# Attention before a mixture of experts: values held stationary in 64-column tiles, softmax weights streamed, sums added up on VectorE

## The chip, the cores and the metric

The kernel runs on one core of one Trainium2 chip. The metric is the device time in microseconds of one execution; the time before is the median of three runs. Times inside the kernel come from one profiled execution.

## What is computed

Eight batches of 448 tokens, twelve heads of 64, then a layer of eight experts that gives each token to one of them; all in float32.

```python
# attention: q, k, v are (8, 12, 448, 64)
scores = scale * np.matmul(q, k.transpose(0, 1, 3, 2))
scores = cap * np.tanh(scores / cap)
scores = scores - np.max(scores, axis=-1, keepdims=True)
attn = np.exp(scores)
attn = attn / (np.sum(attn, axis=-1, keepdims=True) + 1e-09)
x = np.matmul(attn, v)                     # then laid out as (3584, 768)
# experts: w_gate (768, 8), w1 (8, 768, 1024), w2 (8, 1024, 768)
logits = x @ w_gate + modality_bias[modality_id]
e_idx = np.argmax(logits, axis=1)          # one expert a token
gate_w = softmax(logits)[token, e_idx]
out[e_idx == e] = gate_w * (np.maximum(x @ w1[e], 0) @ w2[e])
```

## The kernel before

**The work in stages.** The 96 heads are taken as 48 pairs (two heads of a batch; `NP` = 6 pairs a batch). `attention` (L420) runs over the pairs `g` in four steps each, then the experts follow. TensorE holds one operand of a product stationary (`LDWEIGHTS`, in the profile PEld) and streams the columns of the other. A plain float32 product is two records in the profile. A float32r product has one record; so that no precision is lost, an operand is split into a rounded high half (`kh`, `qs`, `qd`) and the rest (`kl`, `kd`, and the lower rows of `qs`), and their products are summed.

**Scores** (`scores`, L532, products at L547). The keys of a head are cut into three blocks of 128 and a last one of 64, and the two last blocks of a pair make a shared one, so a pair has seven units of 128 keys by 448 queries. Keys are stationary. `kr` and `qr` hold q and k twice, in rows 0 to 63 and 64 to 127, so that one product of 128 rows sums two of the terms (high times high, and high times the rest) and a second one adds the third. Three steps make two units each, the fourth step the shared one with three products: 15 products a pair. ScalarE applies tanh (L552) and exp (L553) to 896 columns, or 448 in the last step, into `pt`: 128 keys by 448 queries a unit.

**Values** (`weigh`, L555). One pair later, for each of four chunks of 112 queries: the chunk of `pt` is stationary and the values `va` are streamed, seven float32 products a step, 28 a pair. A row of `va` holds 64 values, 8 columns of gating values and a one, 73 columns in all (the shared unit, L558, streams both heads' 146). So the product gives the output rows, the head's part of the gating logits, and the softmax denominator beside each other. `normalize` (L575) takes four reciprocals of 112 rows (L579), multiplies the outputs into `xs` (L581) and the logits into `lg` (L587), twice a pair.

**Gating values.** For the values of later pairs `later_gate` (L461) multiplies each pair's transposed values `vt` with the gating weights, three pairs ahead; `put_gate_values` (L410) copies the result into `va`.

**The split of q and k** (`prep`, L491, for the next pair, in step 1): VectorE casts and subtracts (L507 to L517).

**Routing** (`route`, L187, at the end of each batch). VectorE adds up the logits of the 12 heads (L191), finds the largest, and counts: the rank of a token within its expert comes from two small products (`rank`, L218 and L219, the second with the sums `before` that the chain makes up to L215). From it come the positions `pos` (L229). GpSimd writes token number and weight `pay` (iota at L233) with four index DMAs a batch into the map `mapd` (L242). `pay` has two buffers (pool `rp`). GpSimd also stores every half batch of `xs` to `xd` (L658). The seventh routing also chooses the first expert (`early_slot`); at pair 44 its rows are fetched through the map (`mt`, L709; `xg`, L716). The first expert's weights are loaded and split between the last pairs' steps (`split_w`, L730: cast on ScalarE at L732, subtraction on VectorE at L733).

**What sets the order.** A planner orders each engine's instructions, except those that `self.pin` keeps where the code puts them. Before, the products of most pairs are free to move. All DMAs of GpSimd stand in one queue and are issued in order.

Of the kernel before, what the change touches and what calls it, by code (L numbers as in the profile page):

```python
# [42 lines left out]
VA = D + E + 1  # L44
KU, KR = 3, 64
NU = 2 * KU + 2
KW = 2 * S + KR
OWN = KU * 128
GE = 2 * E
# [11 lines left out]
HB = 3  # L61
GH = 2 * HB * GE


class Program:
    def __init__(self, tc, qT, kT, v, vT, cap, mod, wgb, mb, w1, w2, out):
        self.tc, self.nc = tc, tc.nc
        self.qT, self.kT, self.v, self.vT = qT, kT, v, vT
        self.cap, self.mod, self.wgb, self.mb = cap, mod, wgb, mb
        self.w1, self.w2, self.out = w1, w2, out  # L70
# [17 lines left out]
    def constants(self, cpool, dram):  # L88
# [6 lines left out]
        make_identity(nc, self.ident)  # L95
        self.capt = cpool.tile([128, 1], F32, name="capt")
# [12 lines left out]

        self.ones = cpool.tile([CP, 512], BF16, name="ones")  # L110
# [32 lines left out]
    def gate_weights(self):  # L143
        self.wgt = self.cpool.tile([128, NP, GE], F32, name="wgt")
        self.load(self.wgt.rearrange("p h e -> p (h e)"), self.wgb)
# [41 lines left out]
    def route(self, b, lg, pool, ps, tok=None):  # L187
# [3 lines left out]
        nc.vector.tensor_reduce(L, lg.rearrange("p c h e -> p c e h"), axis=AX.X, op=ALU.add)  # L191
# [191 lines left out]
    def load_qk(self, pool, g, parts=1):  # L383
        nc = self.nc
        b, hp = divmod(g, NP)
        kr = pool.tile([128, 2, S], F32, name="kr")
        qr = pool.tile([128, 2, S], F32, name="qr")
        step = 2 * S // parts
        for i in range(parts):
            cs = slice(i * step, (i + 1) * step)  # L390
            for t, src in ((kr, self.kT), (qr, self.qT)):
                self.load(t.rearrange("p j s -> p (j s)")[:, cs], src[b, hp][:, cs])
        return kr, qr

    def gate_values(self, vt, hp, ps, pin=False):

        vg = ps.tile([128, 512], F32, name="vg", tag="small")
        for c in range(KU + 1):
            n = slice(c * 2 * E, (c + 1) * 2 * E)
            for r in range(2 if c == KU else 1):  # L400
                m = slice(r * KR, (r + 1) * KR) if c == KU else slice(0, 128)
                keys = slice(c * 128, c * 128 + (KR if c == KU else 128))
                move = self.nc.tensor.matmul(
                    vg[m, n], vt[:, keys], self.wgt[:, hp], start=True, stop=True
                )
                if pin:
                    self.pin(move)
        return vg[:, : NU * E].rearrange("p (c e) -> p c e", c=KU + 1)

    def put_gate_values(self, va, vg):  # L410
        nc = self.nc
        nc.vector.tensor_copy(
            va[:, : 2 * KU, D : D + E].rearrange("p (c j) e -> p c j e", j=2),
            vg[:, :KU].rearrange("p c (j e) -> p c j e", j=2),
        )
        for j in range(2):
            rows = slice(j * KR, (j + 1) * KR)
            nc.vector.tensor_copy(va[rows, 2 * KU + j, D : D + E], vg[rows, KU, j * E : (j + 1) * E])

    def attention(self, qk, first):  # L420
        tc, nc = self.tc, self.nc
        with ExitStack() as st:
            kp = st.enter_context(tc.tile_pool(name="kp", bufs=1))
            ld = st.enter_context(tc.tile_pool(name="ld", bufs=2))
# [3 lines left out]
            rp = st.enter_context(tc.tile_pool(name="rp", bufs=2))  # L428
            ps_s = st.enter_context(tc.tile_pool(name="ps_s", bufs=2, space=PSUM))
            ps_o = st.enter_context(tc.tile_pool(name="ps_o", bufs=2, space=PSUM))  # L430
            ps_v = st.enter_context(tc.tile_pool(name="ps_v", bufs=1, space=PSUM))


            khs, kls, kds = [], [], []
            for i in range(2):
                kh = kp.tile([128, KW], F32R, name=f"kh{i}")
                kl = kp.tile([128, 2, OWN], F32R, name=f"kl{i}")
                kd = kp.tile([128, 2, KR], F32R, name=f"kd{i}")
                nc.gpsimd.memset(kh.bitcast(F32)[:, S : S + KR], 0.0)
                nc.gpsimd.memset(kd.bitcast(F32), 0.0)  # L440
                khs.append(kh)
                kls.append(kl)
                kds.append(kd)

            wg = kp.tile([128, NP, HB, 2, GE], F32R, name="wg")
            nc.gpsimd.memset(wg.bitcast(F32), 0.0)

            def split_gate():
                for i in range(HB):
                    hi, lo = wg[:, i::HB, i, 0], wg[:, i::HB, i, 1]  # L450
                    nc.vector.tensor_copy(hi, self.wgt[:, i::HB])
                    nc.vector.tensor_tensor(lo, self.wgt[:, i::HB], hi, op=ALU.subtract)

            vgts = [kp.tile([128, KU + 1, HB, GE], F32, name=f"vgt{i}") for i in range(NP // HB)]

            def load_vt(g):
                vt = ld.tile([128, S], F32, name="vt" if g >= HB else "vt0", bufs=2 if g >= HB else 1)
                self.load(vt, self.vT[g // NP, g % NP])
                return vt

            def later_gate(g, vt):  # L461

                hp = g % NP
                vh = sp.tile([128, S], F32R, name="vh", bufs=1)
                keep = self.pin if g < 6 else (lambda inst: inst)
                keep(nc.vector.tensor_copy(vh, vt))
                vl = sp.tile([128, S], F32R, name="vl", bufs=1)
                keep(nc.vector.tensor_tensor(vl, vt, vh, op=ALU.subtract))
                if hp % HB == 0:
                    self.vga = ps_v.tile([128, 512], F32, name="vga")  # L470
                last = hp % HB == HB - 1
                w = wg[:, hp].rearrange("p h t e -> p (h t e)")
                keep(nc.tensor.matmul(self.vga[:GH, :S], w, vh, start=hp % HB == 0, stop=False))
                keep(nc.tensor.matmul(self.vga[:GH, :S], w, vl, start=False, stop=last))
                if not last:
                    return

                vgs = sp.tile([GH, S + KR], F32, name="vgs", bufs=1)
                nc.vector.tensor_copy(vgs[:, :S], self.vga[:GH, :S])
                nc.vector.tensor_copy(vgs[:, S:], self.vga[:GH, OWN:S])  # L480
                tp = self.ps_r.tile([128, 512], F32, name="vgp", tag="small")
                for c in range(KU + 1):
                    nc.tensor.transpose(tp[:, c * GH : (c + 1) * GH], vgs[:, c * 128 : (c + 1) * 128], self.ident[:GH, :GH])
                nc.vector.tensor_reduce(
                    vgts[hp // HB].rearrange("p c h e -> p (c h) e"),
                    tp[:, : (KU + 1) * GH].rearrange("p (x t e) -> p x e t", t=2, e=GE),
                    axis=AX.X,
                    op=ALU.add,
                )

            def prep(g):  # L491
                b, hp = divmod(g, NP)
                kr, qr = first if g == 0 else self.load_qk(qk, g)
                va = ld.tile([128, NU, VA], F32, name="va", bufs=3)
                self.load(va.rearrange("p u d -> p (u d)"), self.v[b, hp])

                kh, kl, kd = khs[g % 2], kls[g % 2], kds[g % 2]
                qs = sp.tile([128, 2, S], F32R, name="qs")
                qd = sp.tile([128, S], F32R, name="qd")
                keep = self.pin if g < 2 else (lambda inst: inst)  # L500

                copy = (lambda out, in_: keep(nc.scalar.copy(out, in_) if g == 0 else nc.vector.tensor_copy(out, in_)))
                for jj in ((0, 1),) if g else ((0,), (1,)):
                    js = slice(jj[0], jj[-1] + 1)
                    for j in jj:
                        o = j * (S + KR)
                        keep(nc.vector.tensor_copy(kh[:, o : o + S], kr[:, j]))  # L507
                    copy(qs[:, js], qr[:, js])
                    keep(nc.vector.tensor_tensor(qs[D:, js], qr[D:, js], qs[D:, js], op=ALU.subtract))  # L509
                    for j in jj:  # L510
                        o, r = j * (S + KR + KR), j * KR
                        keep(nc.vector.tensor_tensor(kl[:, j], kr[:, j, r : r + OWN], kh[:, o : o + OWN], op=ALU.subtract))
                for j in range(2):
                    rows = slice(j * D, (j + 1) * D)
                    r, o = OWN * (1 - j), (OWN, S + KR)[j]
                    copy(qd[rows], qr[rows, j])
                    keep(nc.vector.tensor_tensor(  # L517
# [557 lines left out]
```

## Time and the profile before

| | |
|---|---|
| median of three runs | 1003.48 us (999.76 to 1004.63) |
| the profiled execution | 1003.47 us |
| its span | 1001.9 us, 17725 instructions |
| TensorE busy | 976.2 us (97%) |
| weight loads (PEld) | 941.6 us (94%) |
| VectorE busy | 628.6 us (63%) |
| ScalarE busy | 586.5 us (59%) |
| GpSimd busy | 132.9 us (13%) |
| value products L567, 2304 records | 254.6 us, 260 ns each |
| scores L547, keys high, 384 | 152.2 us, 416 ns each |
| attention's first score product | at 10.3 us |
| first score product of pair 47 | at 465.64 us |
| first transpose of the experts' rows | at 474.4 us |

How to read it: "us" beside an instruction is how long it lasted from start to end; successive products overlap, so the time that one costs is the distance to the next start. `[9.81 <-DMA ...]` after a row is the idle time of its engine before it, and what ended that. PE is TensorE's products, PEld its weight loads, DVE VectorE, ACT ScalarE, POOL GpSimd, SP the engine that issues the loads. An operand is written `out<-in`, in the program's names.

### The profile page before, as it was taken

Reading aid. Unit: us, or ns where it says so; the run is one execution under the profiler, and the core shown is the slowest. Engines: PE = TensorE matmul, PEld = TensorE weight load, DVE = VectorE, ACT = ScalarE, POOL = GpSimd, SP = SyncE. Lnnn points to the kernel's source line nnn. Section 1 sums busy time; section 2 is a strip of 40 time slices with the busy share of each in tenths; the row PEclk is TensorE's granted clock in tenths of the full one; section 3 lists DMA queues with packets and bytes.
Section 4 is the critical chain, followed back from the end, with each engine's and each line's share of the span. In section 5 each row is a group of like instructions: output and inputs, shape, how many; then the busy total and the mean of one; then the engine's idle time right before and its main releaser. Section 6 shows DMA issues by size and latency. Waiting matters only on the chain. (4 is left out here: it accounts for less than half of the span.)

```text
span 1001.9 us, 17725 instructions
## 1 busy us (share of the span) xinstructions
PE 976.2 (97%) x6628; PEld 941.6 (94%) x6628; DVE 628.6 (63%) x1632; ACT 586.5 (59%) x762; POOL 132.9 (13%) x150
## 2 busy tenths in 40 slices
PE   6999999999999999998999999999999999999996
PEld 4999999999999989997999999999999999998996
DVE  5788888878888688767854444343434344337763
ACT  4678778777778777787254434443434344335552
POOL 2001011020202002022242020202020202001100
PEclk8999999999999999998999999999999999999999
DMA  5555556566555647576386353635353545447750
GB/s 177 154 202 147 201 200 168 179 142 213 167 192 156 200 162 184 178 169 237 73 302 220 126 200 121 211 128 193 134 177 141 181 141 180 142 139 227 253 169 36
DMA packets 61160, 173.38 MB, mean 173 GB/s; under 512 B 10366, under 2 KB 17278, under 8 KB 61056
## 3 DMA queue, kind: packets, MB, share of 16 engines
q1 hardware_dynamic: 51968, 138.97, 44.2%
q0 software_dynamic: 8944, 33.10, 10.0%
q8 instruction: 56, 0.92, 0.4%
q14 instruction: 48, 0.39, 0.1%
q10 hardware_dynamic: 144, 0.00, 0.0%
HBM read 150.52 MB, written 22.69 MB: 173 GB/s over the span
## 5 line engine op out<-in xcount | busy, mean ns | idle before, releaser
L567 PE MATMUL po<-va,pt 128*112 128x73 f32 x2304 | 254.6, 260 | 0.0
L567 PEld LDWEIGHTS po<-va,pt 128*112 128x112 f32 x2304 | 249.9, 179 | 0.2
L552 ACT ACTIVATE th<-sc,isc 128x896 f32<-128x896 f32 x192 | 175.2, 913 | 100.3 <-PE sc L547 99.5
L553 ACT ACTIVATE pt<-th,cabs 128x896 f32<-128x896 f32 x192 | 181.7, 950 | 5.8
L780 PE MATMUL ph<-x,al 128*128 128x384 f32 (+2 forms) x528 | 166.3, 315 | 0.0
L802 PE MATMUL py<-bh,hh 128*128 128x384 f32 x464 | 159.3, 343 | 1.1 <-ACT hh L786 1.1
L547 PE MATMUL sc<-qs,kh 128*128 128x448 f32 x384 | 152.2, 416 | 7.6 <-DVE qs L509 7.6
L802 PE MATMUL py<-bh,hl 128*128 128x384 f32 x464 | 156.1, 336 | 0.0
L802 PE MATMUL py<-bl,hh 128*128 128x384 f32 x464 | 155.4, 335 | 0.0
L776 PE MATMUL ph<-x,ah 128*128 128x384 f32 x384 | 128.5, 335 | 0.7 <-DVE x L759 0.7
L777 PE MATMUL ph<-x,ah 128*128 128x384 f32 x384 | 128.6, 335 | 0.0
L733 DVE TENSOR_TENSOR bl<-raw,bh 128x768 fp32r<-128x768 f32 x88 | 81.2, 955 | 51.0 <-ACT bh L732 49.9
L547 PE MATMUL sc<-qs,kl 128*128 128x448 f32 x288 | 109.3, 380 | 0.1
L732 ACT CAST bh<-raw 128x768 fp32r<-128x768 f32 x88 | 70.4, 840 | 55.9 <-DMA raw<-in_w_dram 51.4
L780 PEld LDWEIGHTS ph<-x,al 128*128 128x128 f32 x528 | 99.5, 188 | 0.0
L807 ACT ACTIVATE ot<-py,mt 128x384 f32<-128x384 f32 x58 | 33.6, 580 | 103.2 <-PE py L802 55.2
L762 DVE TENSOR_TENSOR x<-ptr,x 128x384 fp32r<-128x384 f32 (+2 forms) x66 | 32.6, 518 | 96.8 <-ACT x L761 96.6
L733 DVE TENSOR_TENSOR al<-raw,ah 128x1024 fp32r<-128x1024 f32 x66 | 78.8, 1222 | 17.4 <-ACT ah L732 17.1
L802 PEld LDWEIGHTS py<-bh,hh 128*128 128x128 f32 x464 | 87.3, 188 | 1.5 <-ACT hh L786 1.4
L802 PEld LDWEIGHTS py<-bl,hh 128*128 128x128 f32 x464 | 87.3, 188 | 0.0
L802 PEld LDWEIGHTS py<-bh,hl 128*128 128x128 f32 x464 | 87.1, 188 | 0.1
L786 ACT ACTIVATE hh<-ph 128x384 fp32r<-128x384 f32 x64 | 30.6, 489 | 94.7 <-PE ph L780 94.7
(167 smaller groups left out, 1397.0 us busy)
## 6 DMA issues: line engine op xcount, KB each, us to landing
raw<-in_w_dram SPq DMA_DIRECT2D x66, 512.0 KB, 4.6
raw<-in_w_dram SPq DMA_DIRECT2D x88, 384.0 KB, 4.8
kr<-in_kT_dram SPq DMA_DIRECT2D x47, 448.0 KB, 3.4
qr<-in_qT_dram SPq DMA_DIRECT2D x47, 448.0 KB, 4.5
va<-in_v_dram SPq DMA_DIRECT2D x48, 292.0 KB, 3.7
vt<-in_vT_dram SPq DMA_DIRECT2D x48, 224.0 KB, 4.1
xd<-xs POOLq DMA_DIRECT2D x16, 672.0 KB, 5.4
mapd<-pay,pos POOLq DMA_INDIRECT x32, 5.3
```

The costliest lines, as they stand in the source:

```text
L547: move = nc.tensor.matmul(sc[:, i, :S], k, q, start=n == 0, stop=n == len(todo) - 1)
L552: nc.scalar.activation(th[:, :n], sc[:, :n, :S], AF.Tanh, scale=self.isc)
L553: nc.scalar.activation(pt[:, units[0] : units[0] + n], th[:, :n], AF.Exp, scale=self.cabs)
L567: nc.tensor.matmul(po[:CP, o0 + j * VA : o0 + (j + 1) * VA], pt[:, j * KU + i, qs_], va[:, 2 * i + j], start=False, stop=j == 1 and i == K ...
L732: a = self.nc.scalar.copy(hi, raw)
L733: b = self.nc.vector.tensor_tensor(lo, raw, hi, op=ALU.subtract)
L762: nc.vector.tensor_tensor(lo, pt[:, :w], hi, op=ALU.subtract)
L776: nc.tensor.matmul(ph[:, :w], hi[:, fs], self.x[:, k, 0, :w], start=first, stop=False)
L777: nc.tensor.matmul(ph[:, :w], hi[:, fs], self.x[:, k, 1, :w], start=False, stop=False)
L780: nc.tensor.matmul(ph[:, :w], lo[:, fs], self.x[:, k, 0, :w], start=False, stop=last)
L802: nc.tensor.matmul(py[:, :HALF], self.h[a][:, f, rows], self.w2s[f][c][:, cs], start=i == 0, stop=i == 3 * FC - 1,)
L807: nc.scalar.mul(ot[:, cs], py[:, :HALF], mt[:, t, 1:2])
```

## The change

The attention stage is rebuilt; the experts keep their code but for two details.

- **Load.** One packed tile a pair, `kq` (128 x 960): head 0 in rows 0 to 63, head 1 in rows 64 to 127; 3 x 128 own keys, 2 x 64 last keys (block-diagonal, the other half zero), 448 queries. The transposed values and the doubled copies of q and k are not loaded. `va` has 64 columns a unit (512 in all), without gating values and ones.
- **Split** (`prep`, L418 of the new kernel). From pair 2 on the high half `hi` is made by a DMA on GpSimd's queue that casts on the way (L428); VectorE makes `lo` by one subtraction of 960 columns (L432).
- **Scores** (L435). Three terms (high-high, low-high, high-low) in 64-row tiles, head 0 in the upper and head 1 in the lower half of the array, 448 columns each; the shared block takes full products. Two steps' products are issued together.
- **Values** (L468, L476). Values stationary: six products with 64 columns a head, in the two halves of the array's columns, and one of 128 columns for the shared unit; 448 columns of `pt` stream in float32. The result `xT` is transposed: features in rows, queries in columns.
- **Denominators.** VectorE adds up the units of `pt` (`add_up`, L448). One pair later `normalize` (L458) sums over the rows by two float32 products with ones, takes a reciprocal of 128 x 448 (L463) and multiplies (L465). `rows_out` (L479) turns the result back by four transposes and a copy into `xs` (L484).
- **Gating** (L486, L496). Every half batch three products of the normalized `xn` with the gating weights, in 32-column tiles; at the end of the batch a copy `gl`, four transposes `lt`, and `route` sums three values a logit instead of twelve.
- **Order and buffers.** All of attention's products are pinned. The loop is two pairs longer (weigh one pair later, normalize two). Pool `rp`, and `pay` with it, has one buffer instead of two. `den`, `tp`, `lt` and `rank` share one PSUM tile. The raw weights have three buffers instead of four, and the transposes of the gathered rows `xg` use float32r.

```diff
             def prep(g):
...
+                kq = first if g == 0 else self.load_kq(qk, g)
+                va = ld.tile([128, VW], F32, name="va")
...
+                if g > 1:
+                    nc.gpsimd.dma_start(hi, self.kq[b, hp])
...
+                    keep(nc.vector.tensor_tensor(lo[:, cs], kq[:, cs], hi[:, cs], op=ALU.subtract))
...
+                for i, (k, q) in enumerate(((hi, hi), (lo, hi), (hi, lo))):
+                    for j in range(n):
+                        rows = slice(j * D, (j + 1) * D) if step < KU else slice(0, 128)
+                        pin(pe.matmul(sc[:, j, :S], k[rows, ks], q[rows, KC2:], start=i == 0, stop=i == 2))
...
+            def add_up(pt):
...
+                nc.vector.tensor_tensor(tot, pt[:, 0:2], pt[:, 2:4], op=ALU.add)
+                nc.vector.tensor_tensor(tot, tot, pt[:, 4:6], op=ALU.add)
...
+                    nc.vector.tensor_tensor(tot[rows, j], tot[rows, j], pt[rows, 2 * KU], op=ALU.add)
...
+            def normalize(xT, tot):
+                den = self.ps_r.tile([128, 512], F32, name="den", tag="small")
+                for j in range(2):
+                    pin(pe.matmul(den[j * D : (j + 1) * D, :S], self.ones1, tot[:, j], start=True, stop=True))
+                rec = rp.tile([128, S], F32, name="rec")
+                nc.vector.reciprocal(rec, den[:, :S])
+                xn = xp.tile([128, S], F32, name="xn", bufs=HB + 1)
+                nc.vector.tensor_tensor(xn, xT[:, :S], rec, op=ALU.mult)
...
+            def weigh_own(xT, pt, va):
+                for i in range(KU):
+                    for j in range(2):
+                        u = 2 * i + j
+                        pin(pe.matmul(
+                            xT[j * D : (j + 1) * D, :S], va[:, u * D : (u + 1) * D], pt[:, u], start=i == 0, stop=False
+                        ))
...
+            def rows_out(hp, xn, xs):
...
+                    pin(pe.transpose(tp[:CP, c * 128 : (c + 1) * 128], xn[:, c * CP : (c + 1) * CP], self.ident))
...
+                    pin(pe.matmul(
+                        self.glog[t * GW : (t + 1) * GW, :S], self.wgt[:, h0 * HB + t], xn,
+                        start=h0 == 0, stop=h0 == NP // HB - 1,
+                    ))
...
-            for g in range(NG + 1):
...
+            for g in range(NG + 2):
...
+                    if step % 2 == 0 and g < NG:
+                        scores(step, pt, *cur[:2])
+                        scores(step + 1, pt, *cur[:2])
...
+                        if g - 2 in state:
+                            xn = normalize(*state[g - 2])
+                        if g - 1 in state:
+                            ppt, pva = state[g - 1]
+                            tot = add_up(ppt)
+                            xT = ps_x.tile([128, 512], F32, name="xT")
+                            weigh_own(xT, ppt, pva)
...
+                            if php == NP - 1:
+                                self.route(pb, logits(), rp, self.ps_r)
...
-            self.nstage = 4
+            self.nstage = 3
```

What that does to the order of the instructions is seen at three places around the first batch's routing. First TensorE's row before the change, at the two rank products (`oh` is the chosen expert of each token, `vga` the gating values, `po` the weighed values, `sc` scores):

```order
L474 MATMUL vga_928<-vl_1075,wg_199 96x448
L558 MATMUL po_1079<-va_776,pt_857 112x146
L567 MATMUL po_1079<-va_776,pt_857 112x73 x5
L218 LDWEIGHTS tri_94
L218 MATMUL rank_978<-oh_970,tri_94 112x32
L567 MATMUL po_1079<-va_776,pt_857 112x73
L547 MATMUL sc_1087<-qs_888,kh1_194 128x448 x2
L547 MATMUL sc_1087<-qd_889,kd1_196 128x448
L219 LDWEIGHTS ones_92
L219 MATMUL rank_978<-before_972,ones_92 112x32
L558 MATMUL po_1079<-va_776,pt_857 112x146
```

And the same place after it (`tp` the transposes to rows, `lt` those of the logits):

```order
L477 MATMUL xT_732<-pt_619,va_569 128x448
L482 MATMUL tp_757<-ident_73,xn_725 112x128 x4
L491 MATMUL glog_541<-xn_580,wgt_200 32x448
L491 MATMUL glog_541<-xn_653,wgt_200 32x448
L491 MATMUL glog_541<-xn_725,wgt_200 32x448
L502 MATMUL lt_769<-ident_73,gl_767 112x96 x4
L232 LDWEIGHTS tri_95
L232 MATMUL rank_794<-oh_786,tri_95 112x32
L233 LDWEIGHTS ones_93
L233 MATMUL rank_794<-before_788,ones_93 112x32
L443 MATMUL sc_823<-hi_716 128x448 x2
```

Before, value products and a step of scores stand between the two rank products; now they stand together, behind the transposes of the logits and ahead of the next pair's first scores.

GpSimd's row before, at the first batch's four index scatters:

```order
L658 DMA xd_73<-xs_228 448x1x384
L658 DMA xd_73<-xs_541 448x1x384
L242 DMA mapd_74<-pay_988,pos_986 31104x2 x4
L233 IOTA pay_2322 112x4
L658 DMA xd_73<-xs_855 448x1x384
```

And after; each `hi` row is the load for one pair:

```order
L428 DMA hi_716<-in_kq_dram 128x960
L428 DMA hi_847<-in_kq_dram 128x960
L561 DMA xd_70<-xs_612 448x1x384
L256 DMA mapd_71<-pay_804,pos_802 31104x2 x4
L247 IOTA pay_1302 112x4
L428 DMA hi_920<-in_kq_dram 128x960
L428 DMA hi_992<-in_kq_dram 128x960
```

Before, GpSimd's queue held the stores, the scatters and the iota of the next routing; now the loads of `hi` stand in it too, and `hi_920` stands behind the scatters and the iota.

VectorE's row before, where the outputs of a pair are normalized:

```order
L579 RECIPROCAL rec_909<-po_866 112x4
L468 TENSOR_TENSOR vl_926<-vt_790,vh_924 128x448
L581 TENSOR_TENSOR xs_541<-po_866,rec_909 112x2x128
L587 TENSOR_TENSOR lg_229<-po_866,rec_909 112x2x16
L412 COPY va_886<-vgt0_201 128x6x8
```

And after, behind the first routing, whose positions are the first row (`tot` is a sum of units; two pairs are under way):

```order
L243 CAST pos_802<-posf_800 112x4
L463 RECIPROCAL rec_854<-den_851 128x448
L451 TENSOR_TENSOR tot_931<-pt_822 128x896
L465 TENSOR_TENSOR xn_856<-xT_732,rec_854 128x448
L484 COPY xs_888<-tp_889 112x4x128
L452 TENSOR_TENSOR tot_931<-tot_931,pt_822 128x896
L455 TENSOR_TENSOR tot_931<-tot_931,pt_822 64x448
L432 TENSOR_TENSOR lo_921<-kq_916,hi_920 128x960
L463 RECIPROCAL rec_927<-den_924 128x448
```

The small operations on 112 rows have given way to wide ones, and the subtraction `lo_921`, which reads the loaded `hi_920`, stands ahead of the next pair's reciprocal.

More of the change, by code (lines that the diff above doesn't have):

```diff
@@ L95, in constants @@
         make_identity(nc, self.ident)
+        self.identr = cpool.tile([128, 128], F32R, name="identr")
+        nc.vector.tensor_copy(self.identr, self.ident)
         self.capt = cpool.tile([128, 1], F32, name="capt")
@@ L380, in slots, with load_kq @@
         return metai
-    def load_qk(self, pool, g, parts=1):
-        nc = self.nc
+    def load_kq(self, pool, g, parts=1):
         b, hp = divmod(g, NP)
[L386 to L418, printed above, removed]
+        kq = pool.tile([128, QK], F32, name="kq")
+        for cs in (slice(0, QK),) if parts == 1 else (slice(0, KC2), slice(KC2, QK)):
+            self.load(kq[:, cs], self.kq[b, hp][:, cs])
+        return kq
     def attention(self, qk, first):
         tc, nc = self.tc, self.nc
+        pe, pin = nc.tensor, self.pin
         with ExitStack() as st:
-            kp = st.enter_context(tc.tile_pool(name="kp", bufs=1))
-            ld = st.enter_context(tc.tile_pool(name="ld", bufs=2))
+            ld = st.enter_context(tc.tile_pool(name="ld", bufs=3))
             sp = st.enter_context(tc.tile_pool(name="sp", bufs=2))
@@ L427, in attention @@
             xp = st.enter_context(tc.tile_pool(name="xp", bufs=2))
-            rp = st.enter_context(tc.tile_pool(name="rp", bufs=2))
+            rp = st.enter_context(tc.tile_pool(name="rp", bufs=1))
             ps_s = st.enter_context(tc.tile_pool(name="ps_s", bufs=2, space=PSUM))
[L430 to L489, printed above, removed]
@@ L491, in prep @@
+            ps_x = st.enter_context(tc.tile_pool(name="ps_x", bufs=2, space=PSUM))
+            ps_g = st.enter_context(tc.tile_pool(name="ps_g", bufs=1, space=PSUM))
             def prep(g):
                 b, hp = divmod(g, NP)
[L493 to L512, printed above, removed]
@@ new lines, in prep @@
+                va = ld.tile([128, VW], F32, name="va")
+                self.load(va, self.v[b, hp])
+                hi = sp.tile([128, QK], F32R, name="hi")
+                lo = sp.tile([128, QK], F32R, name="lo")
+                keep = pin if g < 2 else (lambda inst: inst)
+                if g > 1:
+                    nc.gpsimd.dma_start(hi, self.kq[b, hp])
+                for cs in (slice(0, QK),) if g else (slice(0, KC2), slice(KC2, QK)):
+                    if g < 2:
+                        keep((nc.scalar.copy if cs.start else nc.vector.tensor_copy)(hi[:, cs], kq[:, cs]))
+                    keep(nc.vector.tensor_tensor(lo[:, cs], kq[:, cs], hi[:, cs], op=ALU.subtract))
@@ new lines, in gate, with logits @@
+            def gate(h0, xns):
+                if h0 == 0:
+                    self.glog = ps_g.tile([128, 512], F32, name="glog")
+                for t, xn in enumerate(xns):
+                    pin(pe.matmul(
+                        self.glog[t * GW : (t + 1) * GW, :S], self.wgt[:, h0 * HB + t], xn,
+                        start=h0 == 0, stop=h0 == NP // HB - 1,
+                    ))
+            def logits():
+                gl = rp.tile([HB * GW, S], F32, name="gl")
+                nc.vector.tensor_copy(gl, self.glog[: HB * GW, :S])
+                lt = self.ps_r.tile([128, 512], F32, name="lt", tag="small")
+                w = HB * GW
+                for c in range(C):
+                    pin(pe.transpose(lt[:CP, c * w : (c + 1) * w], gl[:, c * CP : (c + 1) * CP], self.ident[:w, :w]))
+                return lt[:CP, : C * w].rearrange("p (c t x) -> p c x t", c=C, t=HB)[:, :, :E]
@@ L904, in general @@
                     for j in range(2):
                         h = 2 * hp + j
-                        offs = [KU * 128 if j == 0 else 0] + [(0 if j == 0 else 128) + i * 128 for i in range(KU)]
-                        zero = slice(S, S + KR) if j == 0 else slice(0, KR)
-                        keys = slice(0, S) if j == 0 else slice(KR, S + KR)
+                        offs = [OWN] + [i * 128 for i in range(KU)]
+                        zero = slice(OWN + (1 - j) * KR, OWN + (2 - j) * KR)
+                        last = slice(OWN + j * KR, OWN + (j + 1) * KR)
```

288 lines of the change are left out of this document (111 added, 177 removed).

## The prediction

> **What bounds the kernel now.** I read the page first, then busy time by stretches, then the timelines of TensorE, VectorE and GpSimd inside one batch.
>
> ```profile
> span 1001.9 us, 17725 instructions
> ```
> ```profile
> 200.00:300.00 100.00, 99.87 (x797) 95.14 (x795) 83.07 (x272) 78.67 (x86) 12.43 (x13) 1.00 0.59 177
> ```
> The columns of the stretches are length, then busy time (instructions) of PE, PEld, DVE, ACT, POOL, the granted clock, DMA share and GB/s. PE never rests in this stretch of attention, so it sets the pace; but DVE and ACT are at 83% and 79% there: a lighter PE meets them soon. How long a batch of six pairs lasts is read where GpSimd stores each half batch:
>
> ```profile
> 139.16 0.71 POOL L658 DMA_DIRECT2D xd<-xs  x1 [27.30 <-DVE lg L587]
> ...
> 195.60 0.71 POOL L658 DMA_DIRECT2D xd<-xs  x1 [27.26 <-DVE lg L587]
> 204.34 1.51 POOL L242 DMA_INDIRECT mapd<-pay,pos  x1 [8.03 <-DVE rec L579]
> ...
> 220.64 0.13 POOL L233 IOTA pay<- 112x4 int32 x1 [9.81 <-DMA mapd<-pay,pos]
> ...
> 261.09 1.14 POOL L242 DMA_INDIRECT mapd<-pay,pos  x1 [8.02 <-DVE rec L579]
> ...
> 269.65 0.13 POOL L233 IOTA pay<- 112x4 int32 x1 [3.21 <-DMA mapd<-pay,pos]
> ```
> 195.60 - 139.16 = 56.4 us a batch, 9.4 a pair. This is what the change must beat.
>
> **The pair on TensorE.** The start-to-start times of its products:
>
> ```profile
> 301.34 0.41 PE L558 MATMUL po<-va,pt 128*112 128x146 f32 x2
> 301.59 1.31 PE L567 MATMUL po<-va,pt 128*112 128x73 f32 x12
> 302.70 0.45 PE L547 MATMUL sc<-qs,kh 128*128 128x448 f32 x1
> 302.99 0.37 PE L547 MATMUL sc<-qs,kl 128*128 128x448 f32 x1
> 303.19 0.37 PE L547 MATMUL sc<-qs,kh 128*128 128x448 f32 x1
> ```
> ```profile
> 474.50 0.82 PE L752 MATMUL ptr<-ident,xg 128*128 128x128 f32 x6
> ```
> ```profile
> L752 PE MATMUL ptr<-ident,xg x180: 270/273/275, 474.5 to 968.9; 128*128 128x128 f32 x180
> ```
> A plain float32 product is two records: the 146 columns took 0.25 us, 1.71 ns a column, so 448 columns take 0.77. A split (float32r) product of 448 took 0.20, the first after a change of kind 0.09 more. Six transposes took 0.82, so four some 0.45. The new pair, if two 64-row or two 64-column tiles run together: scores 9 tile pairs and 3 full products, 12 x 0.20 = 2.4; six value products and two of the denominators, 4 x 0.77 and half a product at the ends, 3.5; the shared product 0.77; transposes 0.45; gating, three products in 32-column tiles that half overlap, 1.5 every third pair, 0.5; five changes of shape at 0.09, 0.45. Sum 8.1, against 9.4. No row shows two tiles together. If they did not overlap: 21 x 0.20 + 8 x 0.77 + 0.77 + 0.45 + 0.77 + 0.45 = 12.8. I take 8.1, since the tiles share no rows, columns or PSUM range, and keep 12.8 as a rival.
> [...]
>
> **The pair on ScalarE** is unchanged:
>
> ```profile
> L552 ACT ACTIVATE th<-sc,isc 128x896 f32<-128x896 f32 x192 | 175.2, 913 | 100.3 <-PE sc L547 99.5
> L553 ACT ACTIVATE pt<-th,cabs 128x896 f32<-128x896 f32 x192 | 181.7, 950 | 5.8
> ```
> Four of each in a pair (192 / 48): 4 x (0.913 + 0.950) = 7.45 a pair: a floor.
>
> **The pair on VectorE.** Casts, splits of v and the narrow normalization go; two adds of 896 columns, two of 64x448, one subtraction of 960, a copy of 512, a product of 448 and a reciprocal of 448 columns come.
>
> ```profile
> L733 DVE TENSOR_TENSOR al<-raw,ah 128x1024 fp32r<-128x1024 f32 x66 | 78.8, 1222 | 17.4 <-ACT ah L732 17.1
> L468 DVE TENSOR_TENSOR vl<-vt,vh 128x448 fp32r<-128x448 f32 x45 | 27.8, 618 | 2.7 <-DVE vh L466 0.5
> ```
> ```profile
> 90.99 0.18 DVE L579 RECIPROCAL rec<-po 112x4 f32<-112x4 f32 x1 [0.17 <-PE po L567]
> 91.09 0.36 DVE L466 CAST vh<-vt 128x448 fp32r<-128x448 f32 x1
> 91.37 0.42 DVE L581 TENSOR_TENSOR xs<-po,rec 112x256 f32<-112x256 f32 x1
> 91.70 0.18 DVE L587 TENSOR_TENSOR lg<-po,rec 112x32 f32<-112x32 f32 x1
> 91.80 0.62 DVE L468 TENSOR_TENSOR vl<-vt,vh 128x448 fp32r<-128x448 f32 x1
> ```
> From 448 to 1024 columns the time grows by (1222 - 618) / 576 = 1.05 ns a column, and the next instruction starts some 0.08 before the last one ends (lg: 0.18 long, the next after 0.10). So back to back: adds 2 x 1.01 and 0.1 since the second needs the first; 2 x 0.54; subtraction 1.08; product 0.54; copy 0.6: 5.4 us. The reciprocal is the unknown. Four elements held the pipe for 0.10, as long as 32 of lg. If that is their work, one reciprocal is worth 8 ordinary elements: 448 x 8 x 1.05 ns = 3.8 us. If 0.10 is the least that any instruction holds it, the four show nothing, and 448 columns cost from the 0.5 of a product upwards. I take 3.8, because a four that costs what 32 cost is the nearest row there is; the low end goes into a rival. Sum 9.2: VectorE, not TensorE, sets the pair, and six plain pairs take 55.2 against 56.4.
> [...]
>
> **What the routing adds to a batch.** The bare chain, from the last routing, where nothing else runs on DVE:
>
> ```profile
> 484.59 0.88 DVE L191 TENSOR_REDUCE L<-lg 112x32 f32<-112x384 f32 x1
> ...
> 487.90 0.16 DVE L215 TENSOR_TENSOR acc<-before,oh 112x8 bf16<-112x8 bf16 x1
> ...
> 488.86 0.16 DVE L229 CAST pos<-posf 112x4 int32<-112x4 f32 x1
> ```
> Before, pt products and scores stand between the two rank products, and PE never waits for this chain. After, PE has nothing between the logit transposes, the rank products and the next pair's scores: those queue behind DVE. The chain from the reduction to the second rank took 487.90 - 484.59 = 3.3, and 0.6 less for a reduction over 3 instead of 12. Then PE needs 2.2 for two score steps (1.2) and the denominators (1.0) before the next reciprocal can start, and the copy of the logits adds 0.55 on DVE. Together 2.7 + 2.2 + 0.55 = 5.5 us a batch.
>
> **What the queue of GpSimd adds.** From pair 2 on, a load on GpSimd's queue makes the high half of q and k. After each routing the load for the pair three later stands behind four index scatters and an iota, which must wait until they land, since it rewrites what they read.
>
> ```profile
> xd<-xs POOLq DMA_DIRECT2D x16, 672.0 KB, 5.4
> ```
> In the two batches shown, the iota came 220.64 - 204.34 = 16.3 and 269.65 - 261.09 = 8.6 after the first scatter (of that 9.81 and 3.21 waiting for the landing, so that the four scatters alone take 5.4 at best): 12 in the mean. Now nobody minds. Counted from the start of the next pair's scores: positions ready at 1.1 (488.86 + 0.16 - 487.90), first scatter 0.9 later, iota at 14, load of 480 KB in some 5, so the high half is there at 19. On DVE the subtraction that needs it stands ahead of the next pair's reciprocal; its turn comes at about 2.4 + 7.6 = 10. DVE stands still for 9 us (5.6 to 13.3 by the two batches), behind it the reciprocal, the normalized tile and PE's transposes. The seventh routing is worse: the gather for the first expert stands there too.
>
> ```profile
> 432.97 0.99 POOL L242 DMA_INDIRECT mapd<-pay,pos  x1 [8.42 <-DVE early L271]
> ...
> 459.63 1.23 POOL L716 DMA_INDIRECT xg<-xd,mt  x1 [0.30 <-issue]
> ```
> 460.86 - 432.97 = 27.9 before the load may start: at 2 + 28 + 5 = 35 against a turn at 15 to 17, 18 us.
>
> **Smaller edits.** Transposes of the gathered rows in float32r: at the score rate (0.20 / 448) 128 columns would take 0.06 instead of 0.11, 180 x 0.05 = 9 us saved; a float32r product at 0.20 each would lose 16; I take 0, the two loads of weights being alike.
>
> ```profile
> raw<-in_w_dram SPq DMA_DIRECT2D x88, 384.0 KB, 4.8
> ```
> Three weight buffers instead of four: a raw tile is held some 7.2 us (4.8 to land, and a cast and a subtraction of at most 1.2 each), so three pass the 88 of this row and the 66 of L733's in 154 x 7.2 / 3 = 370 us, and the experts alone last from 474.5 to the end at 1001.9: 0.
>
> Fewer bytes a pair: hidden both ways. Two loops more at the end: 5 us on DVE, of which expert work covers part, 4.
>
> **The sum.** The profiled execution took 1003.47 us, 1.6 more than its span, and the median is 1003.48.
>
> ```profile
> L547 PE MATMUL sc<-qs,kh x384: 362/447/742, 10.3 to 472.7; 128*128 128x448 f32 x192
> ```
> ```profile
> 465.64 0.45 PE L547 MATMUL sc<-qs,kh 128*128 128x448 f32 x1
> ```
> Scores start at 10.3 and pairs 0 and 1, still without reciprocals, take 8 each: pair 2 at 26. Then 45 x 9.2 = 414; six routings 6 x (5.5 + 9) = 87; the seventh 5.5 + 18 = 23.5; four weight splits on a full DVE 4 x 1.14 = 4.6. Pair 47 starts at 555 instead of 465.64: 89 later. With 4 for the end, 1003.5 + 93 = 1096, say 1095. Own range 1065 to 1125 (DVE's halt 5.6 to 13.3).
>
> **The rivals.**
> 1. The reciprocal is cheap (below 2.7 us, so that DVE is under PE's 8.1). For it: nothing in the rows tells work from a least time. Against it: 0.10 is no less than what 32 elements took. PE sets the pair, the late load still stops DVE and through it the transposes: 26 + 45 x 8.1 + 6 x 14 + 23 = 497, 32 later, and 4 at the end: 1039. Chance 0.21.
> 2. Tiles do not overlap. PE sets the pair at 12.8 and hides the load's delay: 10 + 47 x 12.8 + 7 x 6.5 = 657, 191 later, and 4: 1199; if only the scores' tiles overlap, 9 x 0.2 a pair less, 1114. Chance 0.08.
> 3. On the other side: VectorE's queue never holds PE. Its place is the subtraction ahead of the reciprocal; it decides where the high half lands by 10 us and the reciprocal is under 2.7. Then only the rank chain is left: 26 + 45 x 8.1 + 7 x 5.5 = 429, 37 earlier, and 4: 971. Against it: four scatters and the load alone need 10.5 from a start at 2. Chance 0.15.
> 4. The load is early but the reciprocal full: 1095 - 54 - 18 = 1023. Chance 0.06.
>
> **How the numbers follow.** The forecast has 0.50. The range 970 to 1125 takes nearly all of it, the first and fourth rival and half of the third, whose terms could as well come out lower: 0.46 + 0.21 + 0.06 + 0.08 = 0.81. A measurement of this kernel can tell about 0.5% from no change. Faster by more is the third rival, 0.15; within 0.5% only where the fourth gains a little more, 0.03; slower 0.82.
>
> **What would show it.** In the profile after: one reciprocal near 3.8 us (0.6 refutes); DVE busiest in attention, PE below 90%; after each routing PE idle some 3 us before the rank products; lo waiting on a DMA for 6 to 13 us once a batch; pairs 9.2 apart otherwise. Tile pairs of scores that start 0.2 apart refute the overlap. A batch shorter than 56.4 refutes the forecast.

## The result and the profile after

The changed kernel takes 1073.72 us (median of 4 runs, 1069.5 to 1079.43) against 1003.29 for the kernel before (four runs here): a ratio of 1.0711, 95% interval 1.0654 to 1.0769. Forecast were 1095, with a range of 970 to 1125. The profiled execution took 1074.64 us.

The head of the page after the change (for each engine busy us, its share of the span and the number of instructions), and the wide reciprocal's group in it (busy us, mean ns of one | idle us before them):

```profile
span 1073.1 us, 14468 instructions
PE 935.8 (87%) x5232; PEld 713.9 (67%) x5232; DVE 693.0 (65%) x978; ACT 566.2 (53%) x759; POOL 148.8 (14%) x191
...
L463 DVE RECIPROCAL rec<-den 128x448 f32<-128x448 f32 x48 | 141.7, 2953 | 27.0 <-PE den L461 26.5
```

TensorE is no longer full, and one reciprocal takes 2.95 us. VectorE's timeline through an undisturbed pair:

```profile
199.90 0.69 DVE L484 COPY xs<-tp 112x512 f32<-112x512 f32 x1
200.50 1.08 DVE L452 TENSOR_TENSOR tot<-tot,pt 128x896 f32<-128x896 f32 x1
201.69 0.62 DVE L455 TENSOR_TENSOR tot<-tot,pt 64x448 f32<-64x448 f32 x1
202.23 1.14 DVE L432 TENSOR_TENSOR lo<-kq,hi 128x960 fp32r<-128x960 f32 x1
203.30 2.94 DVE L463 RECIPROCAL rec<-den 128x448 f32<-128x448 f32 x1
206.27 0.62 DVE L455 TENSOR_TENSOR tot<-tot,pt 64x448 f32<-64x448 f32 x1
206.93 0.62 DVE L465 TENSOR_TENSOR xn<-xT,rec 128x448 f32<-128x448 f32 x1
207.47 1.08 DVE L451 TENSOR_TENSOR tot<-pt 128x896 f32<-128x896 f32 x1
208.46 0.68 DVE L484 COPY xs<-tp 112x512 f32<-112x512 f32 x1
```

From copy to copy 208.46 - 199.90 = 8.56 us, in which VectorE waits for no other engine. On TensorE the same pair and the next, which holds a batch's routing:

```profile
199.13 0.62 PE L482 MATMUL tp<-ident,xn 128*112 128x128 f32 x4 [0.89 <-DVE xn L465]
199.68 0.48 PE L443 MATMUL sc<-hi 64*128 64x448 f32 x2
199.99 0.38 PE L443 MATMUL sc<-hi,lo 64*128 64x448 f32 x2
200.19 0.38 PE L443 MATMUL sc<-lo,hi 64*128 64x448 f32 x2
...
201.91 2.42 PE L472 MATMUL xT<-pt,va 128*64 128x448 f32 x12
204.27 0.47 PE L443 MATMUL sc<-hi 64*128 64x448 f32 x2
...
208.25 0.95 PE L491 MATMUL glog<-xn,wgt 128*32 128x448 f32 x6
210.73 0.55 PE L502 MATMUL lt<-ident,gl 96*112 96x96 f32 x4 [1.53 <-DVE gl L498]
214.35 0.28 PE L232 MATMUL rank<-oh,tri 112*112 112x32 bf16 x1 [3.08 <-DVE oh L223]
214.94 0.18 PE L233 MATMUL rank<-before,ones 112*112 112x32 bf16 x1 [0.31 <-DVE before L228]
215.05 0.74 PE L443 MATMUL sc<-hi 64*128 64x448 f32 x2
215.59 0.57 PE L443 MATMUL sc<-hi,lo 64*128 64x448 f32 x2
215.97 0.57 PE L443 MATMUL sc<-lo,hi 64*128 64x448 f32 x2
```

Two score products lie in each "x2" row and start 0.20 us after the row before: the tiles of a pair run together. The six value products, twelve records, took 204.27 - 201.91 = 2.36, 0.79 for two. The routing pair, 199.68 plus 8.46 to 215.05, lasted 6.9 longer than an undisturbed one: TensorE stands still at the copy `gl` (1.53) and at the rank products (3.08 and 0.31), and its products afterwards start 0.38 apart instead of 0.20. The granted clock (last but two of the columns) in the stretches ahead of that, in it, and behind:

```profile
199.68:208.14 8.46, 7.46 (x44) 3.90 (x43) 8.29 (x9) 7.01 (x9) 0.53 (x1) 1.00 0.50 153
...
214.30:217.60 3.30, 2.94 (x16) 2.08 (x16) 1.48 (x11) 0.95 (x1) 0.74 (x1) 0.50 0.12 49
217.60:219.40 1.80, 1.80 (x8) 0.76 (x8) 0.00 (x1) 1.77 (x3) 1.24 (x2) 0.50 0.01 1
219.40:222.00 2.60, 2.60 (x14) 0.70 (x12) 2.60 (x1) 1.27 (x2) 1.88 (x2) 0.91 0.02 1
```

GpSimd's queue behind the same routing, and the subtraction on VectorE that needs its load:

```profile
216.86 1.00 POOL L256 DMA_INDIRECT mapd<-pay,pos  x1 [6.71 <-DVE pos L243]
...
225.31 0.13 POOL L247 IOTA pay<- 112x4 int32 x1 [3.68 <-DMA mapd<-pay,pos]
225.84 0.58 POOL L428 DMA_DIRECT2D hi<-in_kq_dram  x1 [0.41 <-PE sc L443]
```
```profile
226.56 0.62 DVE L455 TENSOR_TENSOR tot<-tot,pt 64x448 f32<-64x448 f32 x1
231.14 1.16 DVE L432 TENSOR_TENSOR lo<-kq,hi 128x960 fp32r<-128x960 f32 x1 [3.97 <-DMA hi<-in_kq_dram]
232.22 2.95 DVE L463 RECIPROCAL rec<-den 128x448 f32<-128x448 f32 x1
```

The load leaves 9 us after the first scatter; VectorE waits 4.0 for it with the reciprocal behind. Over the whole span the waits of this line came to 44.6 us:

```profile
  DMA hi<-in_kq_dram: 44.6, 17
```

### The profile page after: what moved, and what is told of

Its sections match the earlier page's. It is cut to its first block, busy times and chain, and to the rows that moved or that the text cites. A ratio compares the mean times of both kernels' runs of the same rounds, so it can differ in the third digit from the quotient of the medians.

```text
span 1073.1 us, 14468 instructions
## 1 busy us (share of the span) xinstructions
PE 935.8 (87%) x5232; PEld 713.9 (67%) x5232; DVE 693.0 (65%) x978; ACT 566.2 (53%) x759; POOL 148.8 (14%) x191
## 5 line engine op out<-in xcount | busy, mean ns | idle before, releaser
L445 ACT ACTIVATE th<-sc,isc 128x896 f32<-128x896 f32 x192 | 169.5, 909 | 139.6 <-PE sc L443 135.2
L446 ACT ACTIVATE pt<-th,cabs 128x896 f32<-128x896 f32 x192 | 176.8, 949 | 2.9
L463 DVE RECIPROCAL rec<-den 128x448 f32<-128x448 f32 x48 | 141.7, 2953 | 27.0 <-PE den L461 26.5
L685 PE MATMUL ph<-x,ah 128*128 128x384 f32 x384 | 129.3, 337 | 1.6 <-DVE plan L383 1.5
L472 PE MATMUL xT<-pt,va 128*64 128x448 f32 x576 | 121.0, 556 | 0.0
L689 PEld LDWEIGHTS ph<-x,al 128*128 128x128 f32 x528 | 102.1, 193 | 0.7 <-issue 0.7
L472 PEld LDWEIGHTS xT<-pt,va 128*64 128x64 f32 x576 | 43.8, 147 | 78.2 <-issue 71.2
L443 PE MATMUL sc<-hi 64*128 64x448 f32 (+1 forms) x336 | 93.2, 484 | 2.9 <-ACT th L445 2.3
L482 PE MATMUL tp<-ident,xn 128*112 128x128 f32 x192 | 31.2, 287 | 73.4 <-DVE xn L465 68.2
L482 PEld LDWEIGHTS tp<-ident,xn 128*112 128x112 f32 x192 | 21.0, 138 | 102.7 <-issue 77.9
L721 POOL DMA_INDIRECT out_dram<-ot,mt x29 | 33.1, 1141 | 396.3 <-ACT ot L716 319.5
```

Of the source, the lines that this page charges most:

```text
L443: pin(pe.matmul(sc[:, j, :S], k[rows, ks], q[rows, KC2:], start=i == 0, stop=i == 2))
L445: nc.scalar.activation(th[:, :n], sc[:, :n, :S], AF.Tanh, scale=self.isc)
L446: nc.scalar.activation(pt[:, 2 * step : 2 * step + n], th[:, :n], AF.Exp, scale=self.cabs)
L463: nc.vector.reciprocal(rec, den[:, :S])
L472: pin(pe.matmul(xT[j * D : (j + 1) * D, :S], va[:, u * D : (u + 1) * D], pt[:, u], start=i == 0, stop=False))
L482: pin(pe.transpose(tp[:CP, c * 128 : (c + 1) * 128], xn[:, c * CP : (c + 1) * CP], self.ident))
```

## The experiments

Each run has the kernel before beside it on the same chip; ratios are to that.

**No reciprocal.** `rec` becomes a constant; the division by the true sums is left out.

```diff
-                nc.vector.reciprocal(rec, den[:, :S])
+                nc.vector.tensor_scalar(rec, den[:, :S], 0.0, 1.0 / S, op0=ALU.mult, op1=ALU.add)
```

> Leaves out the reciprocal: rec is the constant 1/448, written by one ordinary operation on the same 128 x 448 denominators (so the rows come out nearly as before). After the change a reciprocal held VectorE for 2.95 us in every pair and an undisturbed pair took 8.46 us. Theory (VectorE sets the pair): the operation takes 0.6, VectorE needs 6.1 a pair, and the pair falls to what TensorE and ScalarE need, 7.4 to 7.8; 45 pairs win 0.8 to 1.5 each: 1005 to 1040 us. Rival (the pair is set by a chain over the engines or by TensorE, and the reciprocal hides beside it): the undisturbed pair stays above 8.2, 1060 to 1073 us.

1022.51 us, ratio 1.0206 (1.0169 to 1.0243). The operation in its place, and TensorE's first rows of two successive pairs:

```profile
L463 DVE TENSOR_SCALAR rec<-den x48: 609/618/626, 28.1 to 493.2; 128x448 f32<-128x448 f32 x48
```
```profile
116.66 0.47 PE L443 MATMUL sc<-hi 64*128 64x448 f32 x2
...
124.03 0.47 PE L443 MATMUL sc<-hi 64*128 64x448 f32 x2
```

124.03 - 116.66 = 7.37 a pair instead of 8.46: VectorE sets the pair through the reciprocal, and 51 us of the whole hang on it even with all waits left in.

**The load one pair earlier.**

```diff
+                hi = sp.tile([128, QK], F32R, name="hi", bufs=3)
...
-                hi = sp.tile([128, QK], F32R, name="hi")
+                hi = load_hi(g) if g < 3 else his.pop(0)
+                if 1 < g < NG - 1:
+                    his.append(load_hi(g + 1))
...
-                if g > 1:
-                    nc.gpsimd.dma_start(hi, self.kq[b, hp])
```

> The load of the high half is issued one pair earlier into a third buffer, so that the load behind the four index scatters is needed a pair later; all else as changed. Theory (VectorE stands still for the late load, 44.6 us in all before the subtraction, and the TensorE clock falls after the stop): the wait of the subtraction falls below 10 us in all, the batch from 65 to 59 or 60, the stop of the seventh routing by some 10 more: 1020 to 1040 us. Rival (the wait only takes up slack that the routing leaves anyway): less than 10 us won, 1063 to 1073.

1029.0 us, ratio 1.0282 (1.0256 to 1.0308). No row of the subtraction waits for `hi` any more. 45 us less: the wait is real, and in the sum as large as its rows. Place by place it is not: the six batches won 35 us on 24.6 us of such waits, the seventh routing 8.4 on 13.5, where the subtraction now waited 6.3 for `kq`.

**The rank products later.** `route` is cut before `rank`; the second half runs in the next pair's last step.

```diff
+        yield
         rank = ps.tile([128, 512], F32, name="rank", tag="small")
...
+                        if later is not None and g <= NG:
+                            next(later, None)
...
-                                self.route(pb, logits(), rp, self.ps_r)
...
+                                later = self.route(pb, logits(), rp, self.ps_r)
+                                next(later)
```

> The two rank products and what follows them in the routing stand a pair later on TensorE, behind the next pair's four score steps; this also puts one load of the high half ahead of the scatters. Theory (TensorE's next scores wait for VectorE's chain of logits): TensorE's wait of 15 to 20 us in all at the rank products goes, the pair with the routing falls from 15.4 to 10 or 11 us, and the halt for the late load goes with it: 1005 to 1030 us. Rival (VectorE is the bound, so the chain's operations cost the same wherever TensorE stands): the pair with the routing stays above 13, 1050 to 1073.

1061.96 us, ratio 1.0616 (1.0591 to 1.0641): too little. The routing pair fell to 11.5 as expected, but the scatters now come a pair later, and the wait for the load grew with them, to 4.8 to 7.5 us in the six batches instead of 2.1 to 4.9:

```profile
  DMA hi<-in_kq_dram: 47.4, 14
```
```profile
240.47 1.07 PE L483 MATMUL tp<-ident,xn 128*112 128x128 f32 x4 [7.50 <-DVE xn L466]
```

The expectation that the order would remove the halt as well was wrong: it only moved to the next load.

**Both.**

> The earlier load (its own run: 1029 us) and the later rank products (1062 us, routing pair 11.5 instead of 15.4) together. Theory (the two waits partly cover each other, so that either one alone leaves or moves the other): the subtraction waits for no load, the pair with the routing takes 11 to 12, six pairs 55 to 56 us, which is VectorE's own work (6 x 8.46 and 4.5 of routing): 995 to 1010 us. Rival (moving the rank products wins nothing of its own): 1022 to 1032.

1015.89 us, ratio 1.0139 (1.0094 to 1.0184), 6 above the range: the routing pair takes 10.83 and most batches 55.9 to 56.7, but in two the load still came late (59.4 and 60.4). The rival is ruled out: once the load is early, the rank products win 13 more.

**Both, and no reciprocal** (the constant again).

> As the run with the earlier load and the later rank products, and it leaves out the reciprocal: the constant 1/448 in its place. Theory (VectorE then sets nothing outside the routing; ScalarE and TensorE need 7.4 a pair): six pairs in 47 to 50 us, 940 to 965 us, that is 45 to 60 less than with the reciprocal. Rival (the reciprocal hides once the waits are gone): less than 20 less.

955.72 us, ratio 0.9544 (0.9502 to 0.9585). The reciprocal is worth 60 us once the waits are small.

**Idle products in the wait.**

```diff
+        if tok is None:
+            for _ in range(16):
+                self.pin(nc.tensor.matmul(self.glog[:, :S], self.ones[:, :128], self.ones[:, :S], start=True, stop=True))
         rank = ps.tile([128, 512], F32, name="rank", tag="small")
```

> Sixteen products of ones that nobody reads stand on TensorE between the logit transposes and the rank products, where it waited 3 us; all else as changed. In the profile after the change the granted clock was 0.51 in the 5 us after that wait and 1.00 elsewhere. Theory (the clock falls because TensorE stood still): the products after it run at 1.00, 0.20 apart instead of 0.37, and six to seven routings win 1 to 2 us each: 1060 to 1068 us. Rival (the clock falls for another reason, or the added products cost as much as they win): clock still near 0.5, 1072 to 1080.

1077.19 us, ratio 1.0775 (1.0735 to 1.0815), no gain. TensorE's rows at the second routing and, last, the filling at the third:

```profile
145.69 3.19 PE L232 MATMUL glog<-ones 112*128 112x448 bf16 x16
...
149.64 0.48 PE L446 MATMUL sc<-hi 64*128 64x448 f32 x2
149.95 0.38 PE L446 MATMUL sc<-hi,lo 64*128 64x448 f32 x2
150.15 0.38 PE L446 MATMUL sc<-lo,hi 64*128 64x448 f32 x2
...
157.21 0.47 PE L446 MATMUL sc<-hi 64*128 64x448 f32 x2
...
210.44 6.00 PE L232 MATMUL glog<-ones 112*128 112x448 bf16 x16
```

Of the first seven fillings five took 3.19 us, 0.20 a product, and fitted into the rest: the pair with the routing took 15.4 as before. The other two ran at half clock in whole or in part (6.00, with 0.50 granted from 211 to 215 us, and 4.47). In all seven the scores behind run 0.20 apart, and the next pair took 7.6 (157.21 - 149.64) instead of 9.0 to 10.4. What that wins is lost at the next wait: VectorE comes to the subtraction sooner, and the load is not there.

```profile
164.32 1.16 DVE L435 TENSOR_TENSOR lo<-kq,hi 128x960 fp32r<-128x960 f32 x1 [4.60 <-DMA hi<-in_kq_dram]
```

At the same place the changed kernel waited 2.92. Between 60 and 460 us these waits came to 31.3 us instead of 24.3, and a batch took 64.9 in the mean with and without the filling. So the half clock here follows TensorE's rest and lengthens the pair behind it by 1.4 to 2.8 us, but with the late load in place it costs the whole nothing. The theory was right on the clock and wrong on the time; the rival's range was met, but in the main for neither of its two reasons.

**Four buffers and plain transposes again.**

> The changed kernel with two of its edits undone: four buffers for the raw weights again, and the gathered rows transposed in plain float32. The stretch from the last pair's first score to the second block of experts is 71 us after the change and 56 before. Theory (these 15 come from the two added loops, through which the last routing ends 36 instead of 22 us after the last pair's first score; buffers and transposes cost nothing): 1069 to 1078 us. Rival (three buffers hold up the first expert's weights): 1055 to 1065.

1071.05 us, ratio 1.0695 (1.0648 to 1.0741): nothing that can be told from the changed kernel.

**The cast by VectorE**, the rest as changed.

```diff
-                if g > 1:
-                    nc.gpsimd.dma_start(hi, self.kq[b, hp])
...
-                    if g < 2:
-                        keep((nc.scalar.copy if cs.start else nc.vector.tensor_copy)(hi[:, cs], kq[:, cs]))
+                    keep((nc.scalar.copy if cs.start else nc.vector.tensor_copy)(hi[:, cs], kq[:, cs]))
```

> The changed kernel with one edit undone: the high half of every pair is cast by VectorE, not loaded by GpSimd's queue. Theory (VectorE sets the pair): the cast of 960 columns adds 0.8 to 1.1 to each undisturbed pair (8.46 to 9.3 or 9.5), and the waits of the subtraction (44.6 us in all) go; the two nearly cancel: 1060 to 1080 us. Rival (VectorE is not the bound outside the halts): undisturbed pairs stay at 8.5 and the halts go, 1020 to 1035.

1048.91 us, ratio 1.0493 (1.0469 to 1.0516), between the two: the cast took 0.65, not 0.8 to 1.1, and the pairs without a routing lie mostly at 8.2 to 9.4, so the halts cost more than the casts.

**Rows instead of columns.** Denominators as 112 x 8, with the earlier load and the later rank products; the runs above pointed to this.

```diff
-                for j in range(2):
-                    pin(pe.matmul(den[j * D : (j + 1) * D, :S], self.ones1, tot[:, j], start=True, stop=True))
...
+                            den[:CP, n : n + 1], tot[:, j, c * CP : (c + 1) * CP], self.ones1[:, :1], start=True, stop=True
...
-                nc.vector.tensor_tensor(xn, xT[:, :S], rec, op=ALU.mult)
+                nc.vector.tensor_copy(xn, xT[:, :S])
```

> The earlier load, the later rank products, and no wide reciprocal, with nothing left out: the denominators come by eight products with one column, the chunk of the sums stationary, as 112 x 8; the reciprocal of these is multiplied where the rows are copied out, and the gating logits are kept apart by head and divided once a batch. Theory (VectorE 5.5 a pair, TensorE 7.4 + 8 x 0.185 - 0.8 = 8.1, ScalarE 7.45; TensorE sets the pair): six pairs in 50 to 53 us, 960 to 985 us, less than both kernels. Rival (the weight loads of the eight small products are not hidden): a pair above 8.6, 990 to 1010.

1039.14 us, ratio 1.0373 (1.0322 to 1.0424): a miss. An undisturbed pair took 8.28, near the 8.1 expected, but one load a batch came late again. Its iota waited 8.96 us for the scatters, and two loads left only then:

```profile
226.87 0.13 POOL L248 IOTA pay<- 112x4 int32 x1 [8.96 <-DMA mapd<-pay,pos]
227.40 1.16 POOL L424 DMA_DIRECT2D hi<-in_kq_dram  x2 [0.40 <-PE sc L452]
```
```profile
231.58 1.16 DVE L441 TENSOR_TENSOR lo<-kq,hi 128x960 fp32r<-128x960 f32 x1 [8.36 <-DMA hi<-in_kq_dram]
```

**The same, cast by VectorE.**

> As the run with the 112 x 8 reciprocals and the later rank products, but the high half is cast by VectorE and not loaded by GpSimd's queue; nothing is left out. In that run an undisturbed pair took 8.28 us and each batch held one halt of 6 to 10 us where the load stood behind the scatters. Theory (the halt is the queue's; VectorE has 2 us a pair to spare for the cast): no halt, six pairs in 53 to 55 us instead of 60 to 64, 975 to 995 us, less than the kernel before. Rival (VectorE becomes the bound again, or the halt has another cause): 1005 to 1040.

992.19 us, ratio 0.9928 (0.9905 to 0.995): under the kernel before by 0.7%, with an interval that leaves out 1, and far under the changed one. No wait for a load is left in the batches (TensorE waits 1.0 us a batch for `gl`), and from the second batch on each takes 53.4:

```profile
PE 947.1 (96%) x5808; PEld 767.2 (77%) x5808; DVE 598.2 (60%) x1032; ACT 563.9 (57%) x759; POOL 131.3 (13%) x145
```

**A shorter end.** As the run before, and the last pair is normalized in the loop in which it is weighed.

> As the run with VectorE's cast, and the last pair is normalized in the same loop as it is weighed, one loop earlier. Theory (the 15 us lost between the last pair's first score and the second block of experts come from the two added loops and the later last routing): 5 to 10 us less than that run. Rival (the end is bound by the weights or by VectorE's splits): within 2 us of it.

992.76 us, ratio 0.9931 (0.9904 to 0.9958): no gain. The last rank product came at 475.17 instead of 475.12, so the number of loops is not what sets the end there; what an earlier last routing would be worth, this run does not show.

**Other tiles for the gathered rows.** As the run with the rows cast by VectorE (992.19), with two score tiles for the transposes.

```diff
-                        self.transpose(k, (ps_s, self.ps_r)[k % 2], ("sc", "small")[k % 2], busy=k < 2)
+                        self.transpose(k, ps_s, "sc", busy=k < 2)
```

> As the run with VectorE's cast (992 us), and the transposes of the first expert's gathered rows go to the two score tiles only, no longer to the tile that they share with the denominators and the turned rows. In that run TensorE waited 4.6 us there between 448 and 455 us, and ran at half clock up to 462. Theory (the shared tile makes TensorE wait, and the half clock follows): 5 to 9 us less, 983 to 988. Rival (TensorE waits for VectorE's splits, whichever tile is used): 990 to 994.

989.76 us, ratio 0.9891 (0.9858 to 0.9925); the interval overlaps that of the run it starts from, so the step itself is unclear. TensorE waited 3.5 us there instead of 4.6.

## Why the prediction was right, and where it was off

**VectorE sets the pair: shown.** A pair of 8.46 falls to 7.37 without the reciprocal. The size was off: 3.8 was taken for one reciprocal, and it held VectorE for 203.30 to 206.27, 2.97. The other terms, 5.4, were met (8.46 - 2.97 = 5.5). The wide reciprocal cost by the element, as taken: 4 elements lasted 0.18, 8 lasted 0.21 (the run with rows), 448 lasted 2.95, (2.95 - 0.18) / 444 = 6.2 ns each, six ordinary columns and not eight. But the rows from which the 8 was read do not show a cost by the element: 4 elements at 6.2 ns are 0.025 us and 32 columns at 1.05 ns are 0.034, so the 0.10 in both was a least time, the other reading. That the 8 came so near was luck.

**The tiles overlap: shown** by rows 0.20 apart and 0.79 for two value products; the second rival falls. TensorE's busy time in the undisturbed pair was 7.46; the 8.1 of the sum less its 0.5 for gating, which this pair has not, is 7.6. The gating products took 0.95 and not 1.5.

**Rank chain and late load: both shown.** 5.5 and 9 were taken for a batch. The routing pairs took 6.9 to 7.7 extra. TensorE's way from the first score to the next reciprocal, 2.2 in the working, took 4.35 at half clock (215.05 to 219.40) and 2.44 at full clock in the run with idle products. The load was mis-sized: its 9 was 19 for the landing less 10 for VectorE's turn. Counted from the same start, 215.05, the high half was there at 16.1 (231.14) and the turn came at 12.1 (226.56 + 0.62), so the wait was 4.0. It was 2.1 to 4.9 in the six batches, so the wait of 6 to 13 us that was named ahead as a sign did not come there; in the seventh it was 13.5 against 18. The first and the third rival fall with the reciprocal's length and the wait of 44.6, the fourth with that wait; the run with the earlier load came near the fourth's price (1029 against 1023).

**The sum.** Pair 47 started at 519.65, 54 later than before and not 89. Pairs 0 and 1 gave 4 of the 35 (21.8 instead of 26), the reciprocal 45 x (9.2 - 8.46) = 33. Everything beyond pairs of 8.46 came to 519.65 - 21.82 - 45 x 8.46 = 117, forecast 87 + 23.5 + 4.6 = 115. That this sum was met is luck, for its parts were others. The seven routing pairs gave 49 (taken: 7 x 5.5 = 38.5) and VectorE's waits for the load from pair 2 on at most 42.5 (taken: 6 x 9 + 18 = 72). The 25 left over stand against 4.6 for the weight splits: 8.46 is the shortest pair and comes at most once a batch, and the other pairs without a routing took more even where no load was late (9.62 from 237.34 us, for one). The half clock behind the halts is one cause of these (0.84 granted in the mean of the pair from 237.34, which follows a halt of 4.95); the rest was not taken apart.

**The end was missed:** 4 was taken; the profiled execution is 1074.64 - 1003.47 = 71.2 longer, and 71.2 - 54.0 = 17 of it comes behind pair 47's first score. From there to the first transposes of the second block of experts it is 71 us (590.84 - 519.65) instead of 56 (521.84 - 465.64). Of these 15, 13 lie ahead of the first expert product (L776 before, L685 after), where TensorE waits for VectorE between the transposes of the gathered rows and then runs at half clock (0.50 granted from 530.67 to 540.00):

```profile
530.67 1.00 PE L661 MATMUL ptr<-identr,xg 128*128 128x128 f32 x6 [2.12 <-DVE xs L484]
534.08 0.60 PE L661 MATMUL ptr<-identr,xg 128*128 128x128 f32 x3 [2.41 <-DVE x L671]
535.84 1.76 PE L461 MATMUL den<-tot,ones 128*64 128x448 f32 x4 [1.16 <-DVE x L671]
537.39 4.09 PE L472 MATMUL xT<-pt,va 128*64 128x448 f32 x12
...
543.02 0.45 PE L685 MATMUL ph<-x,ah 128*128 128x384 f32 x1
```

Before the change:

```profile
476.06 0.77 PE L776 MATMUL ph<-x,ah 128*128 128x384 f32 x3 [0.73 <-DVE x L759]
```

The buffers are not the cause (the run with four of them), and the number of loops is not in the kernel without halts, whose end is as long (70 us); the shared tile is part of it at most. What else is, stays open. The buffers and the transposes cost nothing, as taken: 1071.05 without the two edits, and the weight load of such a transpose took 0.140 us before and 0.142 after in the median.

## What to carry to other kernels

Fewer matrix instructions win nothing where the work that replaces them makes the next engine the bound: here TensorE's pair fell from 9.4 to 7.5 us and VectorE's rose to 8.5, a third of it one reciprocal of values that repeat over 64 rows. Put such a division where few columns hold it (112 x 8 took 0.21 us). A load that has been moved to a queue with waits in it must be followed past each of them: taking away the halt at the rank products alone won 12 us, for it moved the scatters and with them the next load's wait; with the load early, which alone won 45, it won 13 more.

## What had not been expected of the hardware

After halts of TensorE the granted clock was 0.50 for several microseconds: products started 0.38 apart instead of 0.20 from 215.05 until about 219 us, behind rests of 1.53 and 3.08 with four small transposes between them. A rest of 0.89 alone (199.13) left it at 1.00. The length of the rest alone did not decide: in the run with idle products, behind rests of 1.53 to 1.54, the filling ran at full clock in five of the first seven routings and began at half clock in the other two. Full clock came back only some 5.5 us after the products had begun again (214.35): the granted clock was 0.50 up to 219.80 and 1.00 from 220.00 on.
